# Turning dh and w1 as 2-byte elements, and tying loads, turns and folds to the progress of a pass

## The chip, the cores and the metric

The kernel runs on one core of a Trainium2 chip. The metric is the device time of one execution in microseconds (us). A profile is one execution under the profiler, and its span is some 2 us shorter than the time of the same execution measured from outside (1380.1 against 1381.9 us for the kernel before).

## The reference

The workload is the forward and the backward pass of a gated mix of two layers: a 2-D Fourier filter (A) and an MLP with squared ReLU (B). Cut to what matters here:

```python
def _B_ref(x, w1, b1, w2, b2):            # x 2048x1024, w1 1024x3584, w2 3584x1024, all bf16
    h = einsum("bsd,df->bsf", x, w1) + b1
    r = where(h > 0, h, 0)
    h = r * r
    return einsum("bsf,fd->bsd", h, w2) + b2

g = sigmoid((x * gate_w).sum(-1, keepdims=True))
out = g * irfft2(rfft2(x) * W) + (1 - g) * B(x, w1, b1, w2, b2)
# returned: out and the vjp at grad_out: dx, dw_r, dw_i, dw1 (out_4), db1, dw2 (out_6), db2, dgate_w
```

With 2048 tokens, width 1024 and hidden width 3584, each of the six products of the MLP (h; dh; dW2; dW1; the output; dx) is 896 matmuls of 128x128 by 512 columns. The Fourier transforms are matmuls too, and are woven in between.

## The kernel before

The program has three stages, and TensorE (PE) goes through them with hardly a rest (it is busy for 98% of the span):

1. The **h/dh pass**, some 10 to 467 us. For 28 pairs of 128 hidden units it computes h (matmuls into `ph`, weights w1) and dh (matmuls into `pd`, weights w2 turned), four blocks of 512 tokens each. VectorE turns h, dh, w1 and w2 in blocks of 32x32 on the way; h and dh go to DRAM. The first stage of the Fourier transforms ("folds" on VectorE, small matmuls `pk` and `pu`) runs beside it. w2 is loaded and turned once per weight group of 512 hidden units: seven groups, of which the later six are loaded inside the pass.
2. **dW2, then dW1**, to 949 us. Each streams h or dh back from DRAM.
3. **The output, then dx**, to the end. dx streams w1 turned.

A turn moves elements of 4 bytes if its operand is called int32, so two bf16 elements stay together as a pair. This halves the number of elements on VectorE (one turn of a block of dh takes 0.705 us as 512 elements of 4 bytes a row), but a row of the turned matrix then holds two rows of the original, interleaved, and a matmul has to pick every second element. These are the parts that the change touches:

```python
def load_w2(fg, q):                                     # w2 for the next weight group
    w2r = wb.tile([P, D], BF16, name="w2r", tag="w2r", bufs=4)
    rows_ = B_w2.rearrange("(g h q i c) e -> g q h c i e", h=2, q=4, i=32, c=2)[fg, q]
    for h in range(2):
        for c in range(2):
            a = 2 * h + c
            ld(out=w2r[32 * a : 32 * (a + 1), :], in_=rows_[h, c])      # 32 rows, 64 KB

# in the h/dh pass, after the two products of a block of 1024 tokens (cut):
for src, scr, scrT in ((h2T, h2_scr, h2T_scr), (dhT, dh_scr, dhT_scr)):
    stg = wb.tile([P, 32 // 2, 2, 32], I32, name="stg", tag="stg", bufs=3)
    for c in range(2):
        nc.vector.transpose(out=stg[:, :, c, :], in_=src[:, c, :].bitcast(I32).rearrange("p (b i) -> p b i", i=32))
    st(out=scr[fg][:, 16 * sp : 16 * (sp + 1), 2 * pr : 2 * pr + 2, :], in_=stg[:])
    ...
# dW1: the moving operand takes every second element of dh
mm(pw[:], lhsT=xr[t][:, d_ * P : (d_ + 1) * P], rhs=cur[:, t // 2, t % 2 :: 2], ...)
# dx: the moving operand takes every second element of w1 turned
mm(acc[:], lhsT=cur[:, fc, t2::2], rhs=w1b[:, fc // 2, hf * D + fc % 2 : (hf + 1) * D : 2], ...)
```

`ld` issues a DMA from SyncE, `st` one from GpSimd. `after(a, b)` makes instruction a come after b: with a wait, or, when it is called with `NoSync`, in the order of instructions only.

Of the kernel before, what the change touches and what calls it, by code (L numbers as in the profile page):

```python
# [10 lines left out]
P = 128  # L11
BF16 = mybir.dt.bfloat16
# [5 lines left out]
FDT = FP16  # L18
# [109 lines left out]
def kernel(  # L128
# [64 lines left out]
    gatew_bc = pers.tile([P, D], BF16, name="gatew_bc", tag="gatew_bc")  # L193
    b2_bc = pers.tile([P, D], BF16, name="b2_bc", tag="b2_bc")
# [9 lines left out]
    w1T_scr = dram.tile([FC // 2, P, 4, DC, 32], I32, name="w1T_scr")  # L204
# [3 lines left out]
    dh_scr = [dram.tile([P, S // 64, FGC, 32], I32, name=f"dh_scr{i}") for i in range(FG)]  # L208
# [3 lines left out]

# [19 lines left out]
    def one_s1(fb, cf, T, i, xt, kmat):  # L232
        uv = fb.tile([P, 2, H], FDT, name="uv", tag="uv", bufs=2)
        V(out=uv[:, 0, :], in0=xt[:, 0:H], in1=xt[:, H:D], op=ALU.add)
# [13 lines left out]
        nc.scalar.copy(out=f[:, 5, P::-P], in_=f[:, 0:3:2, P])  # L248
        pk = fps.tile([P, 8, P], FP32, name="pk", tag="ps2", bufs=2)
        for b, (row, o) in enumerate(((5, P), (4, 0), (4, P), (5, 0), (3, 0), (3, P), (1, 0), (1, P))):  # L250
            mm(pk[:, b, :], lhsT=f[:, row, o : o + P], rhs=kmat, start=True, stop=True)
# [198 lines left out]
    def fft_out():  # L450
# [8 lines left out]
        for T in range(2):  # L459
            for i in range(NT):  # L460
# [28 lines left out]
                if T == 0 and i % 2 == 1:  # L489
                    fc = 2 * (i - 1)  # L490
                    if fc < FC:
                        ld(
                            out=w2[:, fc : fc + 4, :].rearrange("p (v c) e -> p v (c e)", c=2),
                            in_=B_w2[fc * P : (fc + 4) * P, :].rearrange("(v m c) e -> m v (c e)", c=2, m=P),
                        )
# [9 lines left out]

    f1, f1_s = pool("f1", "right")
# [4 lines left out]
    def source(i, view):  # L511
        src = f1.tile([P, D], BF16, name="src", tag="src", bufs=8)
        ld(out=src[:], in_=view[i])
        return src
# [18 lines left out]
    def vectors(brow, grow):  # L533
        vps = tps.tile([P, 2, FC // 2], BF16, name="vps", tag="tr", bufs=2)
        for c in range(2):
            nc.tensor.transpose(vps[:, c, :], brow[:, c::2], identb[: FC // 2, : FC // 2])
        nc.vector.tensor_copy(out=b1col[:].rearrange("p (v c) -> p c v", c=2), in_=vps[:])
        gps = tps.tile([P, DC], BF16, name="gps", tag="tr", bufs=2)
        nc.tensor.transpose(gps[:], grow[:], identb[:DC, :DC])
        nc.vector.tensor_copy(out=gwcol[:], in_=gps[:])  # L540
# [16 lines left out]
    def first_stage(T, i):  # L557
        km = kf
        if T:
            xs[i] = source(i, go_perm)  # L560
            km = f1.tile([P, P], FDT, name="kg", tag="kg", bufs=2)
            nc.vector.tensor_scalar(out=km[:], in0=kf[:], scalar1=gcol[:, i : i + 1], scalar2=None, op0=ALU.mult)
        one_s1(f1, cf, T, i, xs[i], km[:])

    def first_stage_of_grad():
        for i in range(NT):
            first_stage(1, i)
            yield
        f1_s.close()


    def mlp_in():
# [8 lines left out]
        def hidden(fc, ss, w1g, h2T):  # L581
            ph = mps.tile([P, SW], FP32, name="ph", tag="ph", bufs=2)
            for dc in range(DC):
                mm(ph[:], lhsT=w1g[:, dc, fc % 2 :: 2], rhs=xT[:, dc, ss], start=(dc == 0), stop=(dc == DC - 1))  # L584
            rT = wb.tile([P, SW], BF16, name="rT", tag="rT", bufs=3)
            nc.scalar.activation(rT[:], ph[:], ACT.Relu, bias=b1col[:, fc : fc + 1])  # L586
            nc.scalar.activation(h2T, rT[:], ACT.Square)  # L587
            return rT
# [19 lines left out]
        def turn_w2(fc):  # L608
            w2r = wb.tile([P, D], BF16, name="w2r", tag="w2r", bufs=4)
            ld(out=w2r[:], in_=B_w2.rearrange("(v m c) e -> v c m e", c=2, m=P)[fc // 2, fc % 2])  # L610
# [12 lines left out]
        def load_w2(fg, q):  # L623

            w2r = wb.tile([P, D], BF16, name="w2r", tag="w2r", bufs=4)
            rows_ = B_w2.rearrange("(g h q i c) e -> g q h c i e", h=2, q=4, i=32, c=2)[fg, q]
            for h in range(2):
                for c in range(2):
                    a = 2 * h + c
                    ld(out=w2r[32 * a : 32 * (a + 1), :], in_=rows_[h, c])  # L630
            stg2[q] = w2r
# [16 lines left out]
        for fp in range(FC // 2):  # L648
# [9 lines left out]
            for sp in range(2):  # L658
                cols2 = slice(2 * sp * SW, 2 * (sp + 1) * SW)
                h2T, dhT = (wb.tile([P, 2, 2 * SW], BF16, name=n_, tag=n_, bufs=2) for n_ in ("h2T", "dhT"))  # L660
                for sh in range(2):
# [9 lines left out]
                    for c in range(2):  # L671
                        if fp > 0:
                            rT = {c: hidden(2 * fp + c, ss, w1g, h2T[:, c, hs])}
                        last = grads(2 * fp + c, sb, ss, rT[c], dhT[:, c, hs])
                        if step == 4:
                            st1 = wb.tile([P, 4, DC, 32], I32, name="stg1", tag="stg1", bufs=1)
                            turned_ = nc.vector.transpose(
                                out=st1[:].rearrange("p b c i -> p c b i"),
                                in_=w1g[:].bitcast(I32).rearrange("p c (b i) -> p c b i", i=32),
                            )  # L680
                            after(turned_, last, mybir.DependencyClass.NoSync)
                            st(out=w1T_scr[fp], in_=st1[:])
                        if pr == 0 and step == 1 and fg > 0:
                            move((2, 3))
                        if fg + 1 < FG:
                            at = 8 * pr + step
                            if at == (9 if fg == 0 else 5):
                                for q in range(4):
                                    load_w2(fg + 1, q)
                            if at == (12 if fg == 0 else 11):  # L690
# [6 lines left out]
                for src, scr, scrT in ((h2T, h2_scr, h2T_scr), (dhT, dh_scr, dhT_scr)):  # L697
                    stg = wb.tile([P, 32 // 2, 2, 32], I32, name="stg", tag="stg", bufs=3)
                    for c in range(2):
                        nc.vector.transpose(  # L700
                            out=stg[:, :, c, :], in_=src[:, c, :].bitcast(I32).rearrange("p (b i) -> p b i", i=32)
                        )
                    st(out=scr[fg][:, 16 * sp : 16 * (sp + 1), 2 * pr : 2 * pr + 2, :], in_=stg[:])
                    st(out=scrT[2 * fp : 2 * fp + 2, :, cols2].rearrange("c p s -> p c s"), in_=src[:])
# [5 lines left out]
        pb1 = tps.tile([FC // 2, 2, P], BF16, name="pb1", tag="tr", bufs=2)  # L710
        for c in range(2):
            nc.tensor.transpose(pb1[:, c, :], gb1b[:, c::2], identb[:])
        gb1r = wb.tile([FC // 2, P, 2], BF16, name="gb1r", tag="gb1r")
        nc.vector.tensor_copy(out=gb1r[:], in_=pb1[:].rearrange("v c m -> v m c"))
        st(out=out_5.rearrange("(v r) -> v r", r=2 * P), in_=gb1r[:].rearrange("v m c -> v (m c)"))
# [15 lines left out]
    def mlp_grads():  # L731
# [5 lines left out]
        def group(scr, fg):  # L737
            t_ = strm.tile([P, NT // 2, 4, FGW // 4], I32, name="grp", tag="strm", bufs=2)
# [5 lines left out]

        xr = []
# [5 lines left out]
        for n, (scr, fg) in enumerate(jobs):  # L751
# [5 lines left out]
            if scr is h2_scr:  # L757
                for fb_ in range(FGC):
                    wo = wb.tile([P, D], BF16, name="wo2", tag="wo2", bufs=2)
                    for hf in range(NH):  # L760
# [7 lines left out]
                        if n in (2, 3):  # L768
                            x_ = wb.tile([P, D], BF16, name=f"res1_{len(xr)}", tag=f"res1_{len(xr)}")
                            after(ld(out=x_[:], in_=x_perm[len(xr)]), last)  # L770
                            xr.append(x_)
                        yield 3
                    dst = out_6.rearrange("(g h a j c) e -> g a h c j e", h=2, a=4, j=32, c=2)[fg, fb_]
                    for q in range(4):
                        st(out=dst[q // 2, q % 2], in_=wo[32 * q : 32 * (q + 1), :])  # L775
            else:
                for d_ in range(DC):
                    pw = mps.tile([P, FGW], FP32, name="pw", tag="pw", bufs=2)
                    for t in range(NT):
                        mm(  # L780
                            pw[:], lhsT=xr[t][:, d_ * P : (d_ + 1) * P], rhs=cur[:, t // 2, t % 2 :: 2],
# [3 lines left out]
                    for h in range(2):  # L785
                        nc.scalar.copy(  # L786
                            out=wo[:, h * 2 * P : (h + 1) * 2 * P].rearrange("p (a j c) -> p a j c", j=32, c=2),
                            in_=pw[:].rearrange("p (a h c j) -> p h a j c", h=2, c=2, j=32)[:, h],
                        )
# [19 lines left out]
    def mlp_out():  # L809
# [3 lines left out]
        w1T = wp.tile([P, FC // 2, 4, DC * 32], I32, name="w1Tr", tag="w1Tr")  # L813
        w1b = w1T[:].rearrange("p v a r -> p v (a r)").bitcast(BF16)
        w1s = w1T_scr[:].rearrange("v p b c i -> p v b (c i)")
        wb, wbs = pool("m3")
        mps, mpss = pool("mps3", "left", PSUM)
        ld(out=b2_bc[:], in_=B_b2.partition_broadcast(P))
        load = blocks(wb, h2T_scr)
# [43 lines left out]
        for k in range(S // BW):  # L863
# [3 lines left out]
            for t2 in range(BW // P):  # L867
# [14 lines left out]
                for hf in range(NH):  # L882
                    cs = slice(hf * H, (hf + 1) * H)
                    acc = mps.tile([P, H], FP32, name="accg", tag="acc", bufs=4)
                    for fc in range(FC):
                        mm(  # L886
                            acc[:], lhsT=cur[:, fc, t2::2], rhs=w1b[:, fc // 2, hf * D + fc % 2 : (hf + 1) * D : 2],
# [10 lines left out]

    later = {}
# [15 lines left out]
    brow = f1.tile([FC // 2, 2 * P], BF16, name="brow", tag="brow")  # L915
    ld(out=brow[:], in_=B_b1.rearrange("(v r) -> v r", r=2 * P))
    grow = f1.tile([DC, P], BF16, name="grow", tag="grow")
    ld(out=grow[:], in_=gate_w.rearrange("(b p) -> b p", p=P))
# [4 lines left out]
    vectors(brow, grow)  # L923
    for i0 in range(0, NT, 4):
# [12 lines left out]
        for i in range(i0, i0 + 4):  # L937
            first_stage(0, i)
    ld(out=gatew_bc[:], in_=gate_w.partition_broadcast(P))
# [3 lines left out]
    mixed = spread(units, first, 0.2)  # L943
# [57 lines left out]
```

## Time and profile before

| | before |
|---|---|
| time, median of 3 (range) | 1382.47 us (1380.53 to 1382.87) |
| span of the profile | 1380.1 us |
| PE busy, granted clock | 98%, full |
| start of dW2, dW1, output, dx | 467.2, 703.6, 949.1, 1166.9 us |
| last matmul of dx | 1369.7 us |

The starts are those of the first matmul of each product in TensorE's timeline. They cut the program into stretches whose lengths can be compared between kernels, and most of what follows is read from them: dW1 takes 949.1 - 703.6 = 245.5 us with the Fourier work in it, dx 202.9 us. The lines that carry the argument stand in the prediction.

### The profile page before, as it was taken

Reading aid. Unit: us, or ns where it says so; the run is one execution under the profiler, and the core shown is the slowest. Engines: PE = TensorE matmul, PEld = TensorE weight load, DVE = VectorE, ACT = ScalarE, POOL = GpSimd, SP = SyncE. Lnnn points to the kernel's source line nnn. Section 1 sums busy time; section 2 is a strip of 40 time slices with the busy share of each in tenths; the row PEclk is TensorE's granted clock in tenths of the full one; section 3 lists DMA queues with packets and bytes.
Section 4 is the critical chain, followed back from the end, with each engine's and each line's share of the span. In section 5 each row is a group of like instructions: output and inputs, shape, how many; then the busy total and the mean of one; then the engine's idle time right before and its main releaser. Section 6 shows DMA issues by size and latency. Waiting matters only on the chain. (4 is left out here: it accounts for less than half of the span.)

```text
span 1380.1 us, 18976 instructions
## 1 busy us (share of the span) xinstructions
PE 1346.1 (98%) x7015; PEld 639.1 (46%) x7149; DVE 709.6 (51%) x1541; ACT 414.2 (30%) x682; POOL 302.0 (22%) x469
## 2 busy tenths in 40 slices
PE   7999999999999999999999999999999999999997
PEld 5654444444444444444444444454555444444443
DVE  6985555465353763455553452234756665632222
ACT  6764444444433222322322223343222000000000
POOL 0223223223322343334322221111101000000000
PEclk9999999999999999999999999999999999999999
DMA  7768887877999778889685668765888845735330
GB/s 276 258 225 230 251 241 210 247 205 221 252 262 272 203 204 196 222 204 228 148 186 158 137 153 264 212 220 183 221 228 220 221 136 157 205 104 147 100 89 23
DMA packets 234584, 273.33 MB, mean 198 GB/s; under 512 B 18400, under 2 KB 175100, under 8 KB 234492
## 3 DMA queue, kind: packets, MB, share of 16 engines
q1 hardware_dynamic: 198716, 153.58, 42.9%
q0 software_dynamic: 35776, 118.54, 28.4%
q8 instruction: 56, 0.92, 0.3%
q14 instruction: 36, 0.29, 0.1%
HBM read 147.25 MB, written 118.51 MB: 193 GB/s over the span
## 5 line engine op out<-in xcount | busy, mean ns | idle before, releaser
L584 PE MATMUL ph<-xT,w1g 128*128 128x512 bf16 x874 | 214.1, 382 | 1.7 <-DMA w1g<-in_B_w_dram 0.4
L594 PE MATMUL pd<-dbT,w2T 128*128 128x512 bf16 x871 | 209.5, 379 | 1.4
L780 PE MATMUL pw<-grp,res 128*128 128x512 bf16 x871 | 205.9, 387 | 1.2
L886 PE MATMUL accg<-w1Tr,hblk 128*128 128x512 bf16 x878 | 202.1, 387 | 1.2
L763 PE MATMUL pw<-dbn,grp 128*128 128x512 bf16 x874 | 196.2, 379 | 2.8 <-DMA grp<-h_scr 1.7
L845 PE MATMUL acc<-w,hblk 128*128 128x512 bf16 x874 | 196.1, 379 | 2.7 <-DVE bGo L847 1.5
L886 PEld LDWEIGHTS <-hblk 128*128 128x128 bf16 x896 | 86.0, 96 | 117.0
L763 PEld LDWEIGHTS <-grp 128*128 128x128 bf16 x896 | 87.1, 98 | 106.0 <-issue 2.5
L780 PEld LDWEIGHTS <-res 128*128 128x128 bf16 x896 | 85.0, 96 | 109.0
L594 PEld LDWEIGHTS <-w2T 128*128 128x128 bf16 x896 | 87.4, 98 | 103.5 <-DVE w2T L616 0.3
L845 PEld LDWEIGHTS <-hblk 128*128 128x128 bf16 x896 | 87.0, 98 | 101.1 <-issue 1.8
L584 PEld LDWEIGHTS <-w1g 128*128 128x128 bf16 x896 | 86.6, 98 | 97.3 <-issue 1.7
L586 ACT ACTIVATE rT<-ph,b1col 128x512 bf16<-128x512 f32 x112 | 77.2, 689 | 180.6 <-PE ph L584 117.4
L598 DVE SCALAR_TENSOR_TENSOR dhT<-pd,rT 128x512 bf16<-128x512 f32 x112 | 75.1, 670 | 86.7 <-PE pd L594 82.3
L700 DVE STREAM_TRANSPOSE stg<-h2T 128x512 int32<-128x512 int32 x56 | 39.8, 711 | 96.6 <-ACT h2T L587 96.6
L891 DVE TENSOR_TENSOR gxo<-accg,g 128x512 bf16<-128x512 f32 x32 | 22.1, 691 | 117.4 <-PE accg L886 111.5
L767 ACT CAST wo<-pw 128x512 bf16<-128x512 f32 x56 | 32.8, 586 | 163.6 <-PE pw L763 141.6
L786 ACT CAST wo<-pw 128x256 bf16<-128x256 f32 x112 | 36.3, 376 | 139.4 <-issue 86.1
L317 DVE CAST x<-px 128x1024 f16<-128x1024 f32 x16 | 19.6, 1224 | 109.4 <-PE px L316 109.4
L775 POOL DMA_DIRECT2D out_dram<-wo x112 | 56.4, 517 | 78.9 <-ACT wo L767 69.8
L587 ACT ACTIVATE h2T<-rT 128x512 bf16<-128x512 bf16 x112 | 70.7, 631 | 3.4
L790 POOL DMA_DIRECT2D out_dram<-wo x56 | 30.8, 549 | 145.9 <-ACT wo L786 145.4
(179 smaller groups left out, 1432.6 us busy)
## 6 DMA issues: line engine op xcount, KB each, us to landing
h2T_scr<-h2T POOLq DMA_DIRECT2D x28, 512.0 KB, 3.6
h_scr<-stg POOLq DMA_DIRECT2D x28, 512.0 KB, 6.3
dhT_scr<-dhT POOLq DMA_DIRECT2D x28, 512.0 KB, 7.7
dh_scr<-stg POOLq DMA_DIRECT2D x28, 512.0 KB, 7.2
grp<-h_scr SPq DMA_DIRECT2D x112, 128.0 KB, 5.5
grp<-dh_scr SPq DMA_DIRECT2D x112, 128.0 KB, 4.5
hblk<-h2T_scr SPq DMA_DIRECT2D x8, 1792.0 KB, 13.4
hblk<-dhT_scr SPq DMA_DIRECT2D x8, 1792.0 KB, 8.8
```

Source lines behind the costliest of these rows:

```text
L584: mm(ph[:], lhsT=w1g[:, dc, fc % 2 :: 2], rhs=xT[:, dc, ss], start=(dc == 0), stop=(dc == DC - 1))
L586: nc.scalar.activation(rT[:], ph[:], ACT.Relu, bias=b1col[:, fc : fc + 1])
L587: nc.scalar.activation(h2T, rT[:], ACT.Square)
L594: mm(pd[:], lhsT=w_[:, ec // 2, ec % 2 :: 2], rhs=dbT[:, ec, ss], start=(ec == 0), stop=(ec == DC - 1),)
L598: return STT(out=dhT, in0=pd[:], scalar=2.0, in1=rT[:], op0=ALU.mult, op1=ALU.mult, accum_out=gb1part[:, fc, sb : sb + 1],)
L700: nc.vector.transpose(out=stg[:, :, c, :], in_=src[:, c, :].bitcast(I32).rearrange("p (b i) -> p b i", i=32))
L763: mm(pw[:], lhsT=cur[:, t // 2, 2 * fb_ * P + t % 2 : 2 * (fb_ + 1) * P : 2], rhs=dbn[:, t, hf * H : (hf + 1) * H], start=(t == 0), stop=( ...
L775: st(out=dst[q // 2, q % 2], in_=wo[32 * q : 32 * (q + 1), :])
L780: mm(pw[:], lhsT=xr[t][:, d_ * P : (d_ + 1) * P], rhs=cur[:, t // 2, t % 2 :: 2], start=(t == 0), stop=(t == NT - 1),)
L786: nc.scalar.copy(out=wo[:, h * 2 * P : (h + 1) * 2 * P].rearrange("p (a j c) -> p a j c", j=32, c=2), in_=pw[:].rearrange("p (a h c j) -> ...
L845: mm(acc[:], lhsT=cur[:, fc, t2::2], rhs=w2[:, fc, cs], start=(fc == 0), stop=(fc == FC - 1))
L886: mm(acc[:], lhsT=cur[:, fc, t2::2], rhs=w1b[:, fc // 2, hf * D + fc % 2 : (hf + 1) * D : 2], start=(fc == 0), stop=(fc == FC - 1),)
```

## The change

Its intent: all operands that matmuls stream become contiguous, and the loads, turns and folds that share the h/dh pass are tied to its progress, so that none runs ahead and gets in the way. Cut to its core:

```diff
-    def load_w2(fg, q):
+    def load_w2(fg, q, last):
             w2r = wb.tile([P, D], BF16, name="w2r", tag="w2r", bufs=4)
-            rows_ = B_w2.rearrange("(g h q i c) e -> g q h c i e", h=2, q=4, i=32, c=2)[fg, q]
-            for h in range(2):
-                for c in range(2):
-                    a = 2 * h + c
-                    ld(out=w2r[32 * a : 32 * (a + 1), :], in_=rows_[h, c])
+            after(ld(out=w2r[:], in_=B_w2.rearrange("(g a q i) e -> g q a i e", a=4, q=4, i=32)[fg, q]), last)
 ...
-    st1 = wb.tile([P, 4, DC, 32], I32, name="stg1", ...)          # w1
+    st1 = wb.tile([P, 2, 4, DC, 32], BF16, name="stg1", ...)
 ...
+    stg = wb.tile([P, 4, 8, 2, 32], BF16, name="stgd", tag="stg", bufs=3)      # dh; h stays I32
+    for c in range(2):
+        nc.vector.transpose(out=stg[:, :, :, c, :].rearrange("p b k i -> p k b i"),
+                            in_=dhT[:, c, :].rearrange("p (k b i) -> p k b i", b=4, i=32))
 ...
-    rhs=cur[:, t // 2, t % 2 :: 2]                                 # dW1
+    rhs=cur[:, t]
-    rhs=w1b[:, fc // 2, hf * D + fc % 2 : (hf + 1) * D : 2]        # dx
+    rhs=w1T[:, fc, 2 * hf : 2 * hf + 2, :]
 ...
     def first_stage_of_grad():
-        for i in range(NT):
-            first_stage(1, i)
+        for n in range(NT + 4):
+            if n < NT:
+                xs[n] = source(n, go_perm, later["last"])          # load, after the last multiply of dh
+            ...                                                    # folds of tile n - 3, matmuls of tile n - 4,
+            ...                                                    # both ordered after that multiply too
```

Left out are the same change of order in b1, the stores of dW2 and the reloads of dh, and a shift of the steps at which w2 is loaded and turned in the first group.

## The prediction

> **What bounds the kernel now.** I read the page's table of engines first, then the groups of matmuls, TensorE's timeline where two of these groups meet, the chain of waits, and last VectorE and the queues in the stretch that the change loads more heavily.
>
> ```profile
> PE 1346.1 (98%) x7015; PEld 639.1 (46%) x7149; DVE 709.6 (51%) x1541; ACT 414.2 (30%) x682; POOL 302.0 (22%) x469
> ...
> PEclk9999999999999999999999999999999999999999
> ...
> L780 PE MATMUL pw<-grp,res 128*128 128x512 bf16 x871 | 205.9, 387 | 1.2
> L886 PE MATMUL accg<-w1Tr,hblk 128*128 128x512 bf16 x878 | 202.1, 387 | 1.2
> L763 PE MATMUL pw<-dbn,grp 128*128 128x512 bf16 x874 | 196.2, 379 | 2.8 <-DMA grp<-h_scr 1.7
> L845 PE MATMUL acc<-w,hblk 128*128 128x512 bf16 x874 | 196.1, 379 | 2.7 <-DVE bGo L847 1.5
> ```
>
> TensorE is busy for 98% of the span at the full clock, so time is won by making its instructions shorter, by removing some, or from the 34 us in which it is idle (1380.1 - 1346.1). Six groups of 896 matmuls with 512 columns make up nearly all of it (a few records are missing, hence 871 to 878). Four of them read their moving operand from contiguous elements; two, L780 (dW1, moving operand dh) and L886 (dx, moving operand w1 turned), read every second 2-byte element, because dh and w1 were turned as 4-byte pairs. Those two have 387 ns per record, the others 379. Records overlap, so the rate must come from distances between starts:
>
> ```profile
> 700.18 3.62 PE L763 MATMUL pw<-dbn,grp 128*128 128x512 bf16 x16
> 703.64 3.79 PE L780 MATMUL pw<-grp,res 128*128 128x512 bf16 x16
> 707.26 0.38 PE L313 MATMUL px<-pm,amat 128*128 128x512 f16 x1
> ```
>
> Sixteen contiguous matmuls take 703.64 - 700.18 = 3.46 us, or 216 ns each; sixteen with the step of two take 707.26 - 703.64 = 3.62 us, or 226 ns. Both have bf16 operands and stand side by side, so the step alone is the likely cause. L763 reads its weights with a step of two and still runs at 216, so a step in the weights costs nothing here. The chain, in its last part, gives the same for L886:
>
> ```profile
> 1270.21 12.07 issue
> 1282.90 12.07 issue
> 1295.60 12.07 issue
> ```
>
> Here "issue" is TensorE going on with nothing to wait for: one tile of 128 tokens, 56 matmuls, every 12.69 us, or 226.6 ns each. The view of TensorE's waits adds up to 15 us over the whole program, most of it in the first 100 us (PE is busy 88.4 of them), and the tail after the last matmul is about 8 us (1380.1 - 1372). The change reaches neither.
>
> [...]
>
> **The change, part by part.**
>
> (a) dh and w1 are turned as 2-byte elements. L780's moving operand becomes eight runs of 64 contiguous elements, L886's 512 contiguous ones. L313 already reads runs of 128 from z at 216 ns, so I expect 216 for both. Gain: L780 896 x (226.3 - 215.8) = 9.4 us, L886 896 x (226.6 - 215.8) = 9.7 us. All of it lies on the path, as TensorE waits for nothing there: -19 us.
>
> (b) The weights of the h/dh pass, b1 and the stores of dW2 also become contiguous. Their weight loads (98 ns) lie beside 216 ns matmuls: 0. One transpose, one small load and a few copies fall away: under 0.5 us.
>
> (c) VectorE pays: 56 dh turns go from 0.705 to about 1.24 us (+30), 14 w1 turns from 1.24 to about 2.4 (+16); busy time goes from 710 to about 755 us. It is not the bound, but in the h/dh pass it empties PSUM: h and dh alternate in two buffers, so dh of the next step (8 matmuls, 1.73 us) may only start once the multiply L598 of this step is done. A step is 3.45 us, and L598 may finish up to 1.73 us after its matmuls. The fullest step of before is this:
>
> ```profile
> 398.58 0.65 DVE L598 SCALAR_TENSOR_TENSOR dhT<-pd,rT 128x512 bf16<-128x512 f32 x1
> ...
> 399.17 2.48 DVE L636 STREAM_TRANSPOSE stg<-w2r 128x512 int32<-128x512 int32 x4
> 401.58 0.67 DVE L700 STREAM_TRANSPOSE stg<-dhT 128x512 int32<-128x512 int32 x1
> 402.17 0.65 DVE L598 SCALAR_TENSOR_TENSOR dhT<-pd,rT 128x512 bf16<-128x512 f32 x1
> ```
>
> From one L598 to the next: 3.59 us. In the new order of instructions this step holds 0.59 + 2.41 (w2) + 1.13 (dh) = 4.13 us in three of the six weight groups, and with an h turn of 0.6 before it 4.73 us in the other three. The second L598 then ends 4.73 + 0.65 = 5.38 us after the first began, where 3.45 + 1.73 = 5.18 is allowed: 0.2 to 0.3 us lost, three times, so 1 us. The step with a first-stage fold of the gradient (some 2.8 us, dh 1.13, multiply 0.6) holds about 4.6 us, but in the new order of TensorE's instructions the FFT's 16 matmuls (1.4 us) lie in the same step: 4.85 us, no loss. In the first 100 us, where VectorE is busy for 82.8, the longer turns add some 3 us, against which one or two folds move later: +0.5. The last dh turn stands before the sum of gb1, for which TensorE already waits 1.1 us: +0.5.
>
> (d) w2 is loaded for turning by one load of 256 KB instead of four of 64 KB, and the load waits for the pass's progress. As built, its source has a slowest dimension of 4[...].
>
> ```profile
> 100.00:400.00 300.00, 297.99 (x1504) 142.12 (x1534) 157.60 (x388) 139.33 (x231) 91.38 (x107) 1.00 0.83 234
> ...
> w2r<-in_B_w_dram SPq DMA_DIRECT2D x96, 64.0 KB, 3.2
> ```
>
> Four such loads put 128 rows of 2 KB on each of the 4 engines; such packets took 84 ns (median) to 110 (mean), so 11 to 14 us alone, and with 0.83 of the engines busy (second number from the end of the first row) more like 20 to 30. Between the issue and the turns lie six steps (6 x 3.45 + 2 = 23 us), in the first group four and much FFT work (about 20 us). So it is close: in some of the six groups the turns may wait a few us in VectorE's queue, with L598 behind them. Estimate: 3 us in all, uncertain from 0 to 25.
>
> (e) dh's reloads become 4 KB rows instead of 512 B: less queue time where no queue is on the path, 0. Merging ScalarE's two copies L786 into one saves it some 9 us, hidden: 0.
>
> Sum: -19 - 0.5 + 1 + 0.5 + 0.5 + 3 = -14.5 us, so 1382.5 - 14.5 = 1368; I take 1367, as loads and turns tied to progress may also spare a short wait.
>
> **The rivals.** First: the 4-engine load holds VectorE and then TensorE in each weight group. For it: the queues are 83% busy and the margin is nil. Against it: six steps of lead, and turn q waits for its own load only. At 4 us each it would make 1388, at 8 us over 1410. Second: VectorE becomes the bound of the pass. For it: a step of two turns, w2 and dh, exceeds 3.45 us. Against it: over four steps the work is about 12 of 13.8 us, and PSUM's slack carries a step; each 0.3 us too little in all 56 half-passes would add 17 us, giving 1382. Third: runs of 64 still cost something, or the step of two was only half the cause: then half of (a) remains, 1376. Fourth, better than my sum: no load is late and the start gets smoother: 1361. More than that has nowhere to come from, since (a) is 19 us and the other idle time is the start and the tail.
>
> **Range and chances.** A gain of 2% needs 1354.8, some 28 us, more than all of (a): 0.04. Slower by 2% needs 1410, only under the first rival in all groups: 0.03. The rest is within 2%. The range runs from all of (a) and some smoother start (1358) to nearly all of (a) eaten by late loads (1380).
>
> **What would show it.** (a) right: the dW1 and dx groups at 379 ns per record, 16 dW1 matmuls in 3.46 us, and tiles of the dx pass 12.1 us apart instead of 12.69. (c) right: 2-byte dh turns of 1.2 us, VectorE near 755 us, no wait of dh's matmuls for L598 over 1 us. (d): w2r's time to landing well above 3.2 us, and any idle of VectorE before the w2 turns released by a DMA; a wait there of more than 2 us in every group makes the prediction wrong, as does a dW1 or dx pass that keeps 226 ns.

A paragraph, and a clause of (d) that rested on it, are cut from the recorded text, as they told things that no profile of this case shows. No term of the sum goes with them: it came to -14.5 us on record and still does. What the paragraph read from the trace before was this. Turns of 512 elements a row took 0.67 to 0.71 us and turns of 1024 (w1g) 1.24 us, so (c) lets the time of a turn grow with the number of its elements. And the 691 loads of the hardware queue have 11046 completion packets of 4 bytes, which is 16 each but for 10 in all, just what two loads with 14 and 8 rows lack to 16. I read that as one completion for each DMA engine that a load uses. That the single load of w2 would use 4, which (d) and the first rival reckon with, was my estimate from the slowest dimension of its source. The trace after shows it in the same count: while the first four of these loads run (82.6 to 101.4 us, with no other load in the queue), it has their 512 packets of 2 KB and 16 completions, 4 a load.

## The result, and the profile after

| | before | after |
|---|---|---|
| time, median (range) | 1382.57 us (1380.53 to 1382.87), 4 runs | 1378.08 us (1376.28 to 1380.01), 4 runs |
| ratio of the times | | 0.9971, 95% interval 0.9954 to 0.9988 |
| span of the profile | 1380.1 us | 1374.2 us |
| start of dW2 | 467.2 | 480.6 (+13.4) |
| start of dW1 | 703.6 | 716.9 (+13.3) |
| start of the output | 949.1 | 953.6 (+4.5) |
| start of dx | 1166.9 | 1171.0 (+4.1) |
| last matmul of dx | 1369.7 | 1364.2 (-5.6) |

The time fell by 4.5 us, inside the predicted range but well short of the predicted 15. The table shows at once where to look: the dW1 and the dx stretch give 8.8 and 9.7 us, as forecast, and the h/dh pass takes 13.4 us more. About 2 of these were forecast for VectorE and 3 for the load of w2.

First the page of the kernel after, lines of the engines and of the groups (line, engine, operation, operands, shapes, count, busy us, mean ns of one, idle before):

```profile
PE 1339.7 (97%) x7146; PEld 643.0 (47%) x7146; DVE 750.9 (55%) x1541; ACT 409.7 (30%) x626; POOL 291.3 (21%) x469
...
L800 PE MATMUL pw<-grd,res 128*128 128x512 bf16 x896 | 200.2, 379 | 0.0
L907 PE MATMUL accg<-w1Tr,hblk 128*128 128x512 bf16 x896 | 193.6, 379 | 0.0
L705 DVE STREAM_TRANSPOSE stgd<-dhT 128x1024 bf16<-128x1024 bf16 x56 | 68.7, 1228 | 0.7
```

Both groups went from 387 to 379 ns, VectorE is at the forecast load (750.9 us, forecast 755), and a dh turn takes the forecast 1.2 us. Next, TensorE's timeline after, where dW2 and dW1 meet:

```profile
713.49 3.62 PE L783 MATMUL pw<-dbn,grp 128*128 128x512 bf16 x16
716.94 3.62 PE L800 MATMUL pw<-grd,res 128*128 128x512 bf16 x16
720.39 0.38 PE L315 MATMUL px<-pm,amat 128*128 128x512 f16 x1
```

Sixteen matmuls of dW1 now take 720.39 - 716.94 = 3.45 us, the same as those of dW2. In the chain of waits, tiles of dx are 1281.56 - 1269.48 = 12.08 us apart, before 12.69:

```profile
1269.48 11.46 issue
...
1281.56 11.46 issue
```

So the gain is there in full. The loss shows in the h/dh pass, at two places. The first is its hand-over from the first weight group, at 82 to 97 us. ScalarE's timeline after:

```profile
86.09 0.63 ACT L586 ACTIVATE h2T<-rT 128x512 bf16<-128x512 bf16 x1
89.35 1.01 ACT L260 CAST u<-pu 128x1024 f16<-128x1024 f32 x1 [2.63 <-DMA z_scr<-u]
90.26 1.02 ACT L255 CAST ft<-pk 128x1024 f16<-128x1024 f32 x1
```

The bracket is the idle time before the instruction and what ended it: in this program ScalarE may not overwrite a buffer of `u` until the store of an earlier `u` to DRAM has read it. The stores issued at 82.15 and 85.45 us landed after 7.1 and 7.5 us; before, the stores of the same stretch took 3.3 to 4.7 us. Just ahead of them, from 81.17 us on, SyncE had issued the four new loads of w2. TensorE needs `ft`, and so it stops too, in its timeline after:

```profile
87.49 1.25 PE L593 MATMUL pd<-dbT,w2T 128*128 128x512 bf16 x5 [0.62 <-DVE w2T L615]
91.33 1.57 PE L278 MATMUL pu<-cf,ft 128*128 128x256 f16 x8 [2.59 <-ACT ft L255]
92.70 1.48 PE L593 MATMUL pd<-dbT,w2T 128*128 128x512 bf16 x3
93.98 3.46 PE L583 MATMUL ph<-xT,w1g 128*128 128x512 bf16 x8
```

The wait itself is 2.59 us, but then eight matmuls of h take 3.46 us instead of 1.89. The view by windows tells why. Its columns are the window, its length, the busy time of PE, PEld, DVE, ACT and POOL with counts, the granted clock of TensorE, the share of the DMA engines that is busy, and GB/s. After:

```profile
88.00:91.30 3.30, 0.74 (x4) 0.13 (x2) 0.62 (x1) 1.93 (x2) 0.65 (x2) 0.85 0.52 178
91.30:94.00 2.70, 2.67 (x12) 1.50 (x13) 0.00 (x0) 0.96 (x1) 0.64 (x1) 0.50 0.85 314
94.00:97.30 3.30, 3.30 (x10) 1.18 (x9) 0.70 (x2) 0.05 (x1) 0.56 (x1) 0.52 0.43 169
```

For some 6 us TensorE was granted half its clock. Ten of its 512-column matmuls started 427 ns apart instead of 216, which costs 2.1 us more. Before, the same windows ran at the full clock:

```profile
91.30:94.00 2.70, 2.64 (x18) 1.37 (x16) 2.67 (x11) 2.70 (x7) 0.55 (x1) 1.00 1.01 383
94.00:97.30 3.30, 3.30 (x17) 1.53 (x16) 0.70 (x2) 1.42 (x4) 0.54 (x1) 1.00 0.87 279
```

The second place is the last weight group. TensorE's timeline after:

```profile
425.08 1.89 PE L593 MATMUL pd<-dbT,w2T 128*128 128x512 bf16 x8 [1.17 <-DMA w2T<-stg]
426.81 1.89 PE L583 MATMUL ph<-xT,w1g 128*128 128x512 bf16 x8
430.49 1.89 PE L593 MATMUL pd<-dbT,w2T 128*128 128x512 bf16 x8 [1.80 <-issue]
```

Before, there was no wait here; these products followed each other every 1.73 us:

```profile
423.99 1.89 PE L594 MATMUL pd<-dbT,w2T 128*128 128x512 bf16 x8
425.72 1.89 PE L584 MATMUL ph<-xT,w1g 128*128 128x512 bf16 x8
```

The turned w2 is moved within SBUF by DMAs that SyncE issues, so I read SyncE's own queue (start, time taken by the issues, count). After:

```profile
392.71 0.38 SPq L645 DMA_DIRECT2D w1g<-in_B_w_dram  x1
393.34 11.60 SPq L759 DMA_DIRECT2D grp<-h_scr  x1
```

One issue of a reload of h took 11.60 us, where the eleven after it take 0.5 to 1.5 us each. It stands behind the last four loads of w2, issued at 385.54 to 388.8 us. All that follows in the queue is late by this: the moves of w2 begin at 417.71 us, and TensorE waits for them. (The profile puts the second wait, of 1.80 us, down to "issue"; in runs 5 and 11 below it puts the wait at the same place down to w2T.) The moves begin 8.6 us after VectorE started to turn this w2 (at 409.1 us). Before, no issue was held here, and they began 2.5 us after the turns (399.2 us):

```profile
383.18 12.31 SPq L742 DMA_DIRECT2D grp<-h_scr  x11
401.68 9.73 SPq L646 DMA_DIRECT2D w2T<-stg  x8
```

Everything else in the pass is small. VectorE's turns of w2 never waited for their loads, which was the way that I had predicted the loads would cost time. dh's matmuls waited four times for VectorE, 1.6 us of idle time in all (by the distances of their starts each of the four cost 0.56 us). And at 123 us there is a wait of 1.2 us that comes from the tying: the second fold of the first tile is not tied, the scheduler put it early into VectorE's queue, and there it waited for its source, whose load is tied.

### The profile page after: what moved, and what is told of

The parts are those of the page before. It is cut to its first block, busy times and chain, and to the rows that moved or that the text cites. A ratio compares the mean times of both kernels' runs of the same rounds, so it can differ in the third digit from the quotient of the medians.

```text
span 1374.2 us, 18936 instructions
## 1 busy us (share of the span) xinstructions
PE 1339.7 (97%) x7146; PEld 643.0 (47%) x7146; DVE 750.9 (55%) x1541; ACT 409.7 (30%) x626; POOL 291.3 (21%) x469
## 4 chain that ended last, share of the span: by engine, by line
PE 50%; issue 37%; POOL 4%; DMA 2%; DVE 2%; ACT 1%; SPq 1%; POOLq 0%; DVEq 0%; ACTq 0%
PE pw L783 14%; PE pd L593 12%; PE ph L583 11%; PE pw L800 7%; PE pu L278 1%; DMA w1g<-in_B_w_dram 1%; POOL ax_scr L490 1%; POOL out_dram L809 1%; POOL out_dram L914 1%; POOL out_dram L873 1%; PE pk L251 1%; PE pv L363 1%; DMA z_scr<-u 1%; PE px L318 1%; PE px L317 1%
## 5 line engine op out<-in xcount | busy, mean ns | idle before, releaser
L583 PE MATMUL ph<-xT,w1g 128*128 128x512 bf16 x896 | 221.2, 384 | 1.2 <-ACT rT L585 1.2
L593 PE MATMUL pd<-dbT,w2T 128*128 128x512 bf16 x896 | 212.6, 380 | 5.2 <-issue 1.8
L800 PE MATMUL pw<-grd,res 128*128 128x512 bf16 x896 | 200.2, 379 | 0.0
L907 PE MATMUL accg<-w1Tr,hblk 128*128 128x512 bf16 x896 | 193.6, 379 | 0.0
L787 ACT CAST wo<-pw 128x512 bf16<-128x512 f32 x56 | 32.8, 586 | 164.9 <-PE pw L783 158.9
L795 POOL DMA_DIRECT2D out_dram<-wo x112 | 56.2, 515 | 84.1 <-ACT wo L787 78.3
L805 ACT CAST wo<-pw 128x512 bf16<-128x512 f32 x56 | 32.9, 587 | 132.0 <-PE pw L800 125.7
L705 DVE STREAM_TRANSPOSE stgd<-dhT 128x1024 bf16<-128x1024 bf16 x56 | 68.7, 1228 | 0.7
```

What stands on the lines that cost most here:

```text
L583: mm(ph[:], lhsT=w1g[:, dc, fc % 2 * P : (fc % 2 + 1) * P], rhs=xT[:, dc, ss], start=(dc == 0), stop=(dc == DC - 1))
L593: mm(pd[:], lhsT=w_[:, ec // 2, ec % 2 :: 2], rhs=dbT[:, ec, ss], start=(ec == 0), stop=(ec == DC - 1),)
L705: nc.vector.transpose(out=stg[:, :, :, c, :].rearrange("p b k i -> p k b i"), in_=dhT[:, c, :].rearrange("p (k b i) -> p k b i", b=4, i=32),)
L795: st(out=dst[q], in_=wo[32 * q : 32 * (q + 1), :])
L907: mm(acc[:], lhsT=cur[:, fc, t2::2], rhs=w1T[:, fc, 2 * hf : 2 * hf + 2, :], start=(fc == 0), stop=(fc == FC - 1),)
```

## The experiments

Three theories stood at the start, and the expectations partly name them by these letters. **A**: the single load of w2, which by its completions (4 a load, where a 32-row load before has 16) runs on 4 DMA engines, causes the loss. **B**: the tying itself causes it. **C**: VectorE's longer turns cause it. Twelve kernels ran, each in five rounds against the kernel before, whose medians were 1382.78, 1381.94, 1382.11 and 1382.19 us on different chips; the medians of the kernel before lie within 0.9 us of each other. Some kernels are wrong, because rows end up in the wrong place; the amount of work is then the same.

| run | what it is | us | ratio to before (95%) |
|---|---|---|---|
| control | the kernel after, again | 1375.40 | 0.9953 (0.9939 to 0.9967) |
| 1 | after, w2 in four 32-row loads | 1367.14 | 0.9888 (0.9875 to 0.9902) |
| 2 | after, turns of dh and w1 in 4 bytes (wrong) | 1377.83 | 0.9972 (0.9959 to 0.9984) |
| 3 | layout alone, with the old order | 1364.22 | 0.9863 (0.9848 to 0.9878) |
| 4 | tying alone, with the old layout | 1383.82 | 1.0011 (0.9998 to 1.0023) |
| 5 | after, folds not tied | 1374.46 | 0.9939 (0.9925 to 0.9952) |
| 6 | after, w2 in one load of 128 rows (wrong) | 1369.00 | 0.9906 (0.9893 to 0.9920) |
| 7 | before, with the single load of w2 (wrong) | 1430.53 | 1.0349 (1.0335 to 1.0363) |
| 8 | after, w2 in two 64-row loads | 1446.27 | 1.0465 (1.0451 to 1.0480) |
| 9 | run 3, dW1 with a step of two (wrong) | 1372.29 | 0.9932 (0.9919 to 0.9944) |
| 10 | run 1, the second fold tied too | 1366.48 | 0.9885 (0.9872 to 0.9899) |
| 11 | after, four 32-row loads in the first group only | 1371.20 | 0.9916 (0.9902 to 0.9931) |

**Run 1: the load of w2 in 32-row pieces, everything else as in the kernel after.**

```diff
-            after(ld(out=w2r[:], in_=B_w2.rearrange("(g a q i) e -> g q a i e", a=4, q=4, i=32)[fg, q]), last)
+            for a in range(4):
+                rows_ = B_w2.rearrange("(g a q i) e -> g q a i e", a=4, q=4, i=32)[fg, q, a]
+                after(ld(out=w2r[32 * a : 32 * (a + 1), :], in_=rows_), last)
```

> The changed kernel with one thing undone: each 256 KB load of w2 for turning is issued as four loads of 32 rows again, still tied to the pass's progress, so each may use 16 engines and not 4. Theory A (the 4-engine loads delay the stores and loads of the hand-over at 82 to 97 us, and TensorE idles 2.6 us and then runs at half its clock): ratio to before 0.992 to 0.994, some 5 us under the changed kernel's 1378; stores of u at 82 to 86 us land in under 5 us instead of 7.1 and 7.5, no idle of 2.6 us before pu at 91 us, no stretch at 432 ns per matmul at 93 to 97 us; the idle at 123 us and at 424 us stays. Theory B (the tying itself comes too late) and theory C (the 2-byte turns load VectorE too much): unchanged, 0.997.

It took 1367.14 us, 11 us under the first measurement of the kernel after and 8 us under the control. Both places of loss are gone; I had expected that only the first would go. In the windows of run 1 the clock is full and the idle time small:

```profile
88.00:91.30 3.30, 3.30 (x21) 1.76 (x20) 1.60 (x3) 1.27 (x2) 1.29 (x2) 1.00 1.01 347
91.30:94.00 2.70, 2.65 (x13) 1.26 (x13) 0.03 (x1) 1.86 (x3) 0.56 (x1) 1.00 0.89 322
```

Compared by starts of dh's multiplies on VectorE, run 1 is 5.8 us ahead of the kernel after once the hand-over is done, and 9.1 us ahead after the last group; it stays at 9.1 to 9.2 to the end. So the load of w2 costs 5.8 + 3.3 us in that profile. That is theory A, but not by the way that the prediction gave for it.

**Run 2: the turns of dh and w1 in 4-byte elements again**, laid out in memory as the kernel after needs it, so that its matmuls stay contiguous. out_1 and out_4 are wrong.

```diff
-                stg = wb.tile([P, 4, 8, 2, 32], BF16, name="stgd", tag="stg", bufs=3)
+                stg4 = wb.tile([P, 16, 2, 32], I32, name="stgd", tag="stg", bufs=3)
                 for c in range(2):
-                    nc.vector.transpose(out=stg[:, :, :, c, :].rearrange("p b k i -> p k b i"), in_=dhT[:, c, :]...)
+                    nc.vector.transpose(out=stg4[:, :, c, :], in_=dhT[:, c, :].bitcast(I32)...)
```

> The changed kernel with dh and w1 turned as 4-byte elements into the same buffers and stored by the same DMAs, so dW1 and dx come out wrong on purpose: VectorE's cost of the change is taken away (dh turns 1.23 to 0.7 us, w1 turns 2.3 to 1.24 us), everything else stays. Theory C (longer turns make most of the loss): at least 7 us under the changed kernel, ratio 0.991 or less, and no hold-up at 88 us, as the store queue no longer waits for the turns. Theory A or B: only the waits of dh's matmuls for the multiply of the step before go (four of 0.56 us), so 1 to 3 us under the changed kernel, ratio 0.995 to 0.996.

It took as long as the kernel after, though VectorE had 44 us less to do (707.2 against 750.9 us). The short waits of dh for VectorE vanished, and others grew by as much. TensorE's waits in run 2 (total us, times, longest):

```profile
PE pd L593 <- DMA w2T<-stg: 6.0, 2, 3.0
PE pu L278 <- ACT ft L255: 5.3, 8, 3.3
```

I had expected 1 to 3 us. Compared by starts of dh's multiplies, run 2 is indeed 2.6 us ahead of the kernel after by the last group, mostly in steps of some 0.5 us, one in each group. There it loses 4.4 us, because the moves of w2 come later still, and dW2 starts 1.8 us later than in the kernel after (482.4 against 480.6). So longer turns cost some 2.6 us here, and theory C falls as the main cause: without them both places of loss remain. Run 3 gives the same price in a pass without these places.

**Run 3: the new layout with the order of the kernel before**: nothing tied, w2 in four 32-row loads.

```diff
-        for n in range(NT + 4):
-            if n < NT:
-                xs[n] = source(n, go_perm, later["last"])
-            ...
+        for i in range(NT):
+            xs[i] = source(i, go_perm)
+            ...
+            one_s1(f1, cf, 1, i, folds(f1, xs[i]), kg[:])
 ...
-            after(ld(out=w2r[:], in_=...), last)
+            for a in range(4):
+                ld(out=w2r[32 * a : 32 * (a + 1), :], in_=rows_)
-                            if at == (7 if fg == 0 else 5):
+                            if at == (9 if fg == 0 else 5):
-                            if at == 11:
+                            if at == (12 if fg == 0 else 11):
```

> Only the data layout of the change: 2-byte turns and contiguous operands, with the loads, w2 turns and gradient folds ordered as in the kernel before, and w2 loaded by four loads of 32 rows. Theories A and B (loads on 4 engines and tied too late): no idle at 88, 123 and 424 us; 19 us gained and 2 to 4 us given back to VectorE, 1366 to 1370 us, ratio 0.988 to 0.991. Theory C: VectorE's turns still hold up the pass, 1374 us or more, ratio over 0.994.

This is the fastest kernel, 1364.22 us, correct, 1.4% under the kernel before. Its h/dh pass ends 2.3 us later than before (469.44 against 467.16), dW1 and dx give 8.3 and 9.7 us. The 2.3 us are close to the forecast of 2 for the longer turns, but not all of them are shown to be VectorE's: TensorE's list has two waits for dh's multiply, 0.5 us in all, and about half of the 2.3 us arises in the first 115 us. These three stretches give -15.7 us, the whole time -18.6. Of the rest, 1.6 us lie after the last matmul, where the program ends sooner than before for a reason that was not looked into.

**Run 4: the tying alone**, on the old layout, with w2 in four loads that are tied like the new one. To find room in SBUF it also makes the two broadcast rows in the last stage of the program, as the kernel after does.

```diff
-                    ld(out=w2r[32 * a : 32 * (a + 1), :], in_=rows_[h, c])
+                    after(ld(out=w2r[32 * a : 32 * (a + 1), :], in_=rows_[h, c]), last)
 ...  # and first_stage_of_grad, source, folds, one_s1 as in the kernel after
```

> The kernel before with only the tying: source loads, w2 loads (four of 32 rows, on 16 engines), w2 turns and folds placed as in the changed kernel, 4-byte turns and operands with a step of two as before. Theory B (tying comes too late by itself): 3 to 6 us slower than before, ratio 1.002 to 1.004, with TensorE waiting for w2T at the last weight group and for a source load at the first fold. Theory A or C: within 1.5 us of before, ratio 0.999 to 1.001.

It cost 1.0 us (interval -0.3 to +3.2), but the total hides something. In its profile dW2 starts 5.5 us later than before (472.7 against 467.2), and that delay stays to the end of dx; the stretch after the last matmul is 3.1 us shorter than before (7.3 against 10.4 us), for a reason that was not looked into. The wait of h's matmuls for ScalarE is there too, larger than in the kernel after, and VectorE's second fold again stands just before it, waiting 3.95 us for its source:

```profile
PE ph L590 <- ACT rT L592: 2.9, 1, 2.9
```

The sixteen matmuls after this wait took 5.1 us instead of 3.5. With the wait that is some 4.7 of the 5.5 us. So theory B is true in a smaller part: the tying costs time in the pass by itself, most of it at the one fold that was not tied.

**Run 5: the kernel after with its folds and their sources in the old order**, while the load of w2 stays single and tied.

```diff
-                xs[n] = source(n, go_perm, later["last"])
-                f[i] = folds(f1, xs[i], later["last"])
+            xs[i] = source(i, go_perm)
+            one_s1(f1, cf, 1, i, folds(f1, xs[i]), kg[:])
```

> The changed kernel with the folds and source loads of the gradient ordered as in the kernel before, while the w2 loads stay tied and on 4 engines: is the damage of those loads due to their meeting the tied folds? Theory A1 (the 4-engine loads alone do it): the stores of u near 85 us still land in 7 us and TensorE idles over 1 us there; the w2T moves of the last group are no longer behind the reloads of h, since f1's space is free some 18 us earlier: 1371 to 1377 us, ratio 0.992 to 0.996. If the tied folds are the partner: as the four-loads kernel or better, 1364 to 1368.

1374.46 us against the control's 1375.40. Both places of loss are still there: the reload's issue took 10.4 us, and TensorE waited 4.4 us for w2. So the tied folds don't cause them. (I had expected that the moves of the last group would no longer stand behind the reloads; they still do.)

**Run 6: one load of the same 256 KB, but from 128 consecutive rows**, so that the source's slowest dimension is 128. The rows are the wrong ones.

```diff
-            after(ld(out=w2r[:], in_=B_w2.rearrange("(g a q i) e -> g q a i e", a=4, q=4, i=32)[fg, q]), last)
+            after(ld(out=w2r[:], in_=B_w2[(4 * fg + q) * P : (4 * fg + q + 1) * P, :]), last)
```

> The changed kernel with the w2 loads still single loads of 256 KB, but of 128 consecutive rows, so that they may use 16 engines; the rows are the wrong ones on purpose, so most outputs are wrong. Theory A1 (the number of engines is what costs): as with four loads of 32 rows, 1365 to 1369 us, ratio 0.987 to 0.990. Rival A2 (one big load instead of four small ones is what costs, whatever its engines): like the changed kernel, 1376 to 1380 us.

1369.00 us, within 2 us of run 1. So neither the number of loads nor their size makes the loss. What is left is the shape of the source, and with it the number of engines: the loads of run 6 have 16 completions each, those of the kernel after 4. And the same reloads of h pass SyncE's queue without being held. In run 6, ten of them take less than the first one alone in the kernel after:

```profile
389.47 10.50 SPq L759 DMA_DIRECT2D grp<-h_scr  x10
```

The record of packets, which no view of the profile prints, shows the loads at work. Four loads of w2 are 512 packets of 2 KB in SyncE's queue. Those of the last group take 20 us in the kernel after (387.9 to 408.3 us), 6.5 us in run 6 and 7.8 us in run 1. In the fullest 2 us of this group the kernel after has 4.0 of them under way at a time, in the mean (4.2 in the first group), and the kernel before, with its 32-row loads, 8.6; that fits the counts of completions. While they run in the kernel after, the queue starts no packet of the reloads of h (512 bytes each) from 396.9 to 405.7 us. VectorE's turns of this w2 begin at 409.1 us, 0.8 us after the last packet: the load was as slow as the prediction feared, and just in time.

**Run 7: the kernel before with the single load**, nothing tied (rows wrong).

```diff
-            rows_ = B_w2.rearrange("(g h q i c) e -> g q h c i e", h=2, q=4, i=32, c=2)[fg, q]
-            for h in range(2):
-                for c in range(2):
-                    a = 2 * h + c
-                    ld(out=w2r[32 * a : 32 * (a + 1), :], in_=rows_[h, c])
+            ld(out=w2r[:], in_=B_w2.rearrange("(g a q i) e -> g q a i e", a=4, q=4, i=32)[fg, q])
```

> The kernel before with one thing added: each group of four 32-row loads of w2 replaced by the changed kernel's single load over 4 engines (rows of the changed layout, so wrong results on purpose); no tying, 4-byte turns. Theory A1: 5 to 11 us slower than before, ratio 1.004 to 1.008, with the stores of u near 85 us landing in 7 us and TensorE idle for over 1 us near 90 us. Rival (the load costs only together with the tying or the longer turns): within 2 us of before.

It lost 48 us, far over what I expected. Without the tying, three of the next group's loads go out as soon as their buffers are free, at 112.65 us, and right behind them in SyncE's queue come the moves of w2 that TensorE needs next:

```profile
112.65 3.36 SPq L626 DMA_DIRECT2D w2r<-in_B_w_dram  x3
116.11 24.71 SPq L642 DMA_DIRECT2D w2T<-stg  x16
```

TensorE's timeline and waits in run 7:

```profile
135.63 3.57 PE L594 MATMUL pd<-dbT,w2T 128*128 128x512 bf16 x8 [12.08 <-DMA w2T<-stg]
```

```profile
PE pd L594 <- DMA w2T<-stg: 33.4, 8, 12.1
```

So the tying is what makes the single load bearable: it keeps the loads away from the moves. In run 7 the clock falls as well: the eight matmuls after the wait take 3.57 us instead of 1.89, and the mean granted clock of its profiled run is 0.987 (0.999 before).

**Run 8: two loads of 64 rows**, a slowest dimension of 2.

```diff
+            for a in range(0, 4, 2):
+                rows_ = B_w2.rearrange("(g a q i) e -> g q a i e", a=4, q=4, i=32)[fg, q, a : a + 2]
+                after(ld(out=w2r[32 * a : 32 * (a + 2), :], in_=rows_), last)
```

> The changed kernel with each w2 load split into two of 64 rows, whose slowest dimension is 2, so each may use only 2 engines[...] (a dose). Results stay right. Theory A1: twice the rows on each of half the engines, so the loads take twice as long, some 45 us for 1 MB: the turns then wait in every weight group, 20 to 120 us slower than the changed kernel (1400 to 1500 us). If the number of engines does not matter: 1376 to 1380 us.

1446.27 us. Here the way that the prediction described does appear, VectorE waiting for w2 and TensorE for VectorE:

```profile
PE pd L593 <- DVE dhT L597: 65.7, 6, 12.5
DVE stg L633 <- DMA w2r<-in_B_w_dram: 62.7, 12, 8.9
```

With 16, 4 and 2 engines (counted by completions) the kernel takes 1367 to 1369, 1375 to 1378 and 1446 us; the 512 packets of the first group's loads take 5.6 (run 6), 18.7 and 33.1 us. The predicted wait is real; at 4 engines the lead just covers it.

**Run 9: run 3 with a step of two in dW1's moving operand** (out_4 wrong), to size the first step of the prediction by itself.

```diff
-                return t_[:].rearrange("p a r k x -> p k (a r) x")
+                return t_[:].rearrange("p a r k x -> p (a r) (k x)")
-                            rhs=cur[:, t],
+                            rhs=cur[:, :, 128 * (t // 2) + t % 2 : 128 * (t // 2 + 1) : 2],
```

> The turns-only kernel (1364.2 us) with dW1's moving operand read with a step of two again out of the same buffer (64 elements of every second in eight runs; dW1 wrong on purpose). If the step alone makes 226 ns out of 216: 9 to 10 us slower than turns-only, 1373 to 1374 us, ratio 0.993, and the dW1 group at 387 ns per record. If it was the 4-byte layout or something else: 1364 us.

It cost 8.1 us (1372.29 against 1364.22), and the group is back at the record's length of before:

```profile
L795 PE MATMUL pw<-grd,res 128*128 128x512 bf16 x896 | 209.7, 387 | 0.0
```

**Run 10: run 1 with the second fold tied too.**

```diff
-        V(out=uv[:, 1, :], in0=xt[:, 0:H], in1=xt[:, H:D], op=ALU.subtract)
+        after(V(out=uv[:, 1, :], in0=xt[:, 0:H], in1=xt[:, H:D], op=ALU.subtract), earlier, mybir.DependencyClass.NoSync)
```

> The four-loads kernel e1 with the second half of each fold's first step tied too (in e1 only the first of the two was tied, and the second was placed early in VectorE's queue, where it waited for its load and held TensorE for 0.9 us at 118 us). That hold-up goes: 0.5 to 1.5 us under e1, 1366 us, ratio 0.9875 to 0.989; the four waits of 0.56 us for the w2 turns stay. If the order costs elsewhere: no better than e1.

The wait at 123 us (119 us in run 1) is gone from TensorE's list, but the time is the same as in run 1 within the noise (ratios 0.9885 and 0.9888); the waits of dh for VectorE grew from 1.6 to 2.2 us. Run 3, without any tying, is still 2 to 3 us faster.

**The control: the kernel after, unaltered.**

> The changed kernel unaltered, as a control beside the other two of this call: 1376 to 1380 us, ratio 0.996 to 0.998, with the idle of 2.6 us at 88 us and the late w2T near 424 us again.

1375.40 us (1373.20 to 1378.92), where the first measurement had 1378.08 (1376.28 to 1380.01): the ranges overlap. Its profile repeats both losses: stores of u that take 7.1 and 8.1 us, a wait of 2.53 us, a clock of 0.61 at 91.3 to 94 us, and a reload issue of 11.5 us.

**Run 11: four 32-row loads in the first of the six groups only.**

```diff
+            rows_ = B_w2.rearrange("(g a q i) e -> g q a i e", a=4, q=4, i=32)[fg, q]
+            if fg == 1:
+                for a in range(4):
+                    after(ld(out=w2r[32 * a : 32 * (a + 1), :], in_=rows_[a]), last)
+            else:
+                after(ld(out=w2r[:], in_=rows_), last)
```

> The changed kernel, with the loads of w2 in 32-row pieces (16 engines) for the first of the six later weight groups only; the other five keep the 4-engine load. Theory: the cost of the 4-engine load sits in two places, the hand-over at 82 to 97 us (5.8 us in the profile of the changed kernel against that with all loads in pieces) and the last group at 390 to 431 us (3.3 us), and nowhere between. Then this run gains 4 to 7 us on the changed kernel (1375.4 us in the last call): about 1370 us; the stores of u land within 5 us again, TensorE keeps the full clock at 91 to 97 us, and one issue of a reload of h in SyncE's queue near 390 us still takes over 10 us, with TensorE waiting some 3 us for w2 near 425 us. Rival: each of the six groups pays alike, through slower transfers in general: then the gain is a sixth of 8 to 11 us, 1.5 us or so, and the time is about 1374 us.

1371.20 us, 4.2 us under the control, as the theory said and not the 1.5 us of an equal share. The stores of u land after 4.4 and 5.1 us, and the clock at 91.3 to 97.3 us is full. The last group still pays; in SyncE's queue the first two reloads take 11.11 us, and TensorE waits in run 11:

```profile
389.13 11.11 SPq L764 DMA_DIRECT2D grp<-h_scr  x2
```

```profile
425.43 1.89 PE L593 MATMUL pd<-dbT,w2T 128*128 128x512 bf16 x8 [1.87 <-DMA w2T<-stg]
```

From here to run 1, which spares the other five groups as well, it is another 4.1 us (1371.20 against 1367.14).

## Why the prediction was right or wrong

The time fell into the range (1358 to 1380), but the forecast gain was 15 us and the measured one 4.5, with 7 in the control. That it stayed inside is in part luck: the upper end stood for turns that wait for late loads, and no turn waited. Point by point:

- **(a), the contiguous operands, -19 us: right.** The dW1 and the dx stretch shrank by 8.8 and 9.7 us, 18.5 in all, at the predicted 216 ns per matmul. Run 9 undoes the one half and loses 8.1 us. The third rival (runs of 64 still cost something) falls.
- **(b) and (e), under 0.5 us and 0: not contradicted,** and too small to be seen by themselves.
- **(c), VectorE, +2 us with the two half microseconds: right in size.** The pass of run 3 grew by 2.3 us, and run 2 puts the turns at 2.6 us. Where the time goes was less well seen: the kernel after has four waits of dh for VectorE's multiply, each worth 0.56 us, where I had counted three losses of 0.2 to 0.3. The second rival, VectorE as the bound, falls: with 44 us taken from VectorE, run 2 was no faster.
- **(d), the load of w2: this is the step that failed.** It says "in some of the six groups the turns may wait a few us in VectorE's queue, with L598 behind them", and "Estimate: 3 us in all, uncertain from 0 to 25". The runs show 8 us (run 1 against the control) to 11 us (against the first measurement) in its place, and by another path. The turns did not wait. The estimate of the load itself held: I had put 20 to 30 us on the four loads, and their packets took 19 and 20 us in the first and the last group. I followed the load to its own reader, and asked whether it would land in time; it did, in the last group by 0.8 us. The cost fell on transfers that have nothing to do with w2: the stores of u at the hand-over (about half, run 11), and a reload of h in SyncE's queue, with the moves of w2 behind it, in the last group (the other half, run 1 against run 11). At the hand-over the wait was made dearer by the half clock (0.50 to 0.52) that followed it, by 2.1 us.
- **The tying, for which I took off 1 us ("loads and turns tied to progress may also spare a short wait"): wrong in sign.** Run 3 is 2.9 us faster than run 1, and the pass of run 4 is 5.5 us longer than before (its whole time 1.0 us, within the noise). Its one service was not in my list at all: with the single load it is worth an estimated 40 us, the 48 us of run 7 less the 8 us between run 1 and the control (the layouts of the two pairs differ).

The first rival, a late 4-engine load, named the right part and the wrong mechanism; its sizes of 4 to 8 us in each group apply at 2 engines (run 8, up to 12.5 us for each of six stalls), not at 4.

The profiles tell how much of this lies in the h/dh pass. Its end (the start of dW2) moves by +2.3 us from before to run 3 (layout), +2.0 from there to run 1 (tying), and +9.1 from there to the kernel after (load), together the +13.4 of the table; dW1 and dx give -18.5 back, the rest -0.8, and the spans differ by -5.9. Each step is one pair of profiles. That the parts of such a chain add up proves nothing, as they always do; what counts is where each of them was found. By medians the steps are -18.6, +2.9 and +8.3 us, the last one to the control. It was run at another time.

Three things stay open. The kernel after took 1378.1 us in one call and 1375.4 in the other. Its two profiles differ by 2.6 us: 0.8 us before the first multiply of dh, 1.3 at the hand-over and 0.5 in the last group; why they do is not known, and it may be scatter. That the 4 engines themselves were overfull, and held the stores of u and the reload of h, is inferred from the shape of the source, the counts of completions, the packets of the loads and runs 1, 6 and 8; the trace does not name the engine of a packet. And of the 2.9 us between runs 1 and 3, the profiles put 2.0 into the pass (TensorE waits 0.7 us at 119 us, and 1.6 instead of 0.5 us for VectorE) and 1.3 after the last matmul, with 0.6 the other way between; why the end of the program differs was not traced.

## What to carry to other kernels

When a load is reshaped, ask how many engines it will use (here its completion packets told: 16 a load before, 4 after), and then look at every other transfer issued in the same few microseconds, not only at the load's own reader. Count the issues and waits of the queue itself: here one held issue of 11.6 us delayed all that stood behind it. And when a change bundles a gain with "harmless" reordering, run the parts apart: here run 3, the layout alone, gave 18.6 us, and the bundle 4 to 7.

## What the runs show of the hardware

- A moving operand in bf16 with a step of two ran at 226 to 227 ns per matmul of 512 columns against 216 for a contiguous one, 5% slower; run 9 shows it by itself (8.1 us over 896 matmuls). A step of two in the weights cost nothing (216 ns).
- The 24 loads of w2 lower the completion packets of the hardware queue from the 16 x 619 - 10 of 619 loads by just 24 x 12, to 9606, which is 4 a load; the 48 loads of run 8 fit 2 a load in the same way. What few engines cost others: stores of 256 KB that took 7.1 to 7.5 us instead of 3.3 to 4.7, an issue in SyncE's queue that took 11.6 us instead of 0.5 to 1.5, and in the whole 8 us at 4 engines and 79 at 2 (runs 8 and 1), with 48 us at 4 engines if the loads stand before moves that are needed (run 7).
- In the kernel after, a pause of TensorE of 2.59 us, in a stretch of 3.3 us in which it was busy for 0.74 us, was followed by some 6 us at a granted clock of 0.50 to 0.52; in the control a pause of 2.53 us was followed by 2.7 us at 0.61 and 3.3 us at 0.80. Pauses of 1.80 us (at 428.7 us) and 1.61 us (at 515.2 us) in the kernel after were followed by the full clock (1.00 from 430.5 to 440 and from 516.8 to 525 us). What decides between the two was not shown.
